# Four sends of the first block moved to ScalarE's queue, and the second clearing of spare rows planned behind the mixing weights

## The chip, the cores and the metric

One core of one Trainium2 chip runs the whole kernel. The metric is the device time of one execution in microseconds (us). Before the change the median of three runs is 1155.92 us (1154.21 to 1157.16).

## The reference

Three layers follow each other: attention in which the heads are mixed before and behind the softmax, then two MLPs. All in float32.

```python
scores = scale * np.matmul(q, k.transpose(0, 1, 3, 2))      # 4 batches, 12 heads, 448 x 448, head size 64
scores = np.einsum('bhij,hg->bgij', scores, w_pre)
scores = scores - np.max(scores, axis=-1, keepdims=True)
attn = np.exp(scores)
attn = attn / (np.sum(attn, axis=-1, keepdims=True) + 1e-09)
attn = np.einsum('bhij,hg->bgij', attn, w_post)
out = np.matmul(attn, v)
...
h = x @ w_in;  x = (h * np.cos(h)) @ w_out                  # 1792 tokens, 768 -> 2048 -> 768
h = max(x @ w1, x @ w2, x @ w3);  x = h @ w_out2            # 768 -> 768 -> 768
```

## The kernel before, in words

The attention is cut into 16 blocks of 100 to 120 queries of one batch (10 to 12 slots of ten queries), four blocks to a batch. Block n goes through these steps, by the names of the program:

- `qk` (L553): for each of six pairs of heads TensorE makes scores for the block's queries in two PSUM tiles. In block 0 the pairs take their tiles from three pools in turn, `ps`, `aps` and `mps`; later all take `ps`, which has two.
- `evac` (L461): ScalarE or VectorE copies each head's scores to SBUF, into one of seven tiles `s`, or in block 0 for odd heads into one of six tiles `e`.
- `send` (L567): a DMA puts one head's scores into the block's grid `t`, so that the heads of one query come to lie on neighbouring partitions. There are two grids, used in turn. Twelve sends fill one. Rows that no send writes must be zero: `fill` (L499) clears them once per grid on GpSimd.
- `mix1` (L576): TensorE mixes the heads with the weight `w`. One visit covers two slots (one slot at the end of a block of 11), so a block has five or six visits, and all blocks 92, numbered 0 to 91. A block's first visit needs all twelve of its sends.
- `rowmax` (L584, VectorE), `soft` (L590, ScalarE's exp with the sum), `guard`, `recip` and `wscale` (L595 to L604, VectorE) make the softmax's parts of a visit; the weight of the second mix, `w2t`, takes the reciprocal in.
- `mix2` (L617): TensorE's second mix of a visit, 64 small matmuls; `keep` (L461) copies the result into a tile `a`.
- `av` (L640): for every one or two blocks, the weighted sums of the values, in three parts; `keepx` and `out` (L655) put them to DRAM.

Before all this `wget` (L507, L509) loads the small weights by GpSimd's queue, and `wmix` (L515 to L522) makes `w` (its step 0) and `w2t` (its step 1) from them on VectorE.

Little of the order is written out by hand. `Plan.add` enters each step with a rank, the engines that may do it with a cost for each (T, A, V, P for TensorE, ScalarE, VectorE and GpSimd; D for SyncE's queue), the steps that it comes after, and the buffers that it takes and frees. `Plan.run` then goes through the steps greedily: of those that by its own clock can start soonest it takes the one of lowest rank, on the engine that would be done first, and writes that instruction into the engine's stream. So a cost or a dependence changed at one place can change the order of everything behind it, and which of two engines makes a copy. The semaphores are set from the data that the instructions share: a dependence that only the plan knows makes no wait in the program. Every engine goes through its stream in order.

The first MLP's matmuls begin among the last visits; the MLPs (L157 to L159) follow.

Of the kernel before, what the change touches and what calls it, by code (L numbers as in the profile page):

```python
# [16 lines left out]
B, H, S, D = 4, 12, 448, 64  # L17
# [30 lines left out]
@with_exitstack  # L48
def talking_heads_mlps(ctx, tc, q, k, v, w_pre, w_post, same_row, w_in, w_out, w1, w2, w3, w_out2, outT):
    nc = tc.nc  # L50
    dram = ctx.enter_context(tc.tile_pool(name="dram", bufs=1, space=bass.MemoryType.DRAM))
    xT = dram.tile([DM, NT], F32, name="xT")

    tp = ctx.enter_context(tc.tile_pool(name="t", bufs=2, side="right", reuse_waits="tile"))
    mlps = Mlps(ctx, tc, xT, tp, w_in, w_out, (w1, w2, w3), w_out2, outT)
    mlps.kept = {(i, f): dram.tile([128, DM], F32, name=f"w{i}_{f}") for i in range(3) for f in range(KC)}
    mlps.kept_out = dram.tile([KC, 128, DM], F32, name="w3")
    mlps.kept.update({(3, f): mlps.kept_out[f] for f in range(KC)})
    with tc.manual_schedule(), ExitStack() as att:
        attention(att, tc, q, k, v, w_pre, w_post, same_row, xT, tp, mlps)  # L60
# [384 lines left out]
def attention(ctx, tc, q, k, v, w_pre, w_post, same_row, xT, tp, mlps):  # L445
# [35 lines left out]
    score, halves = [], []  # L481
# [59 lines left out]
    def score_bank(n, hp):  # L541
        grid = lambda: ps_t.tile([128, JB, H, RI], F32, name="aps").rearrange("p j g i -> p (j g i)")[:, :S]
        return (("ps", lambda: ps_x.tile([128, S], F32, name="ps")), ("ps_t", grid),
                ("ps_m", lambda: ps_m.tile([128, S], F32, name="mps")))[hp % 3 if n == 0 else 0]
# [11 lines left out]
    def copy_place(n, h):  # L556
        return ("e", ep) if n == 0 and h in range(1, 2 * BUFS["e"], 2) else ("s", sp)
# [71 lines left out]
    def pairs(x):  # L629
        return 2 * x, 2 * x + 1  # L630
# [28 lines left out]
    def add(f, a, rank, engines, after=(), turn=False, behind=(), **kw):  # L659

        key = f.__name__, *a
        plan.add(key, rank, partial(f, *a), engines, after, behind=list(before.get(f, ()) if turn else ()) + list(behind), **kw)
        if turn:
            before[f] = [key]
# [9 lines left out]
    for x in range(3):  # L674
        add(wget, (x,), -70.0, {"P": 1.1 + 1.1 * (x == 2)}, lands=3.0)
    for n in range(2):
        add(fill, (n,), -60.0, {"P": 5.0})
    add(wmix, (0,), -39.0, {"V": 0.8}, [("wget", 0), ("wget", 2)])
    add(wmix, (1,), -39.0, {"V": 0.2}, [("wget", 1), ("wget", 2)])
    for n in range(NS):  # L680
        b = score[n][0]
        start, end = score[n - 1][0] != b or not n, n == NS - 1 or score[n + 1][0] != b
        for hp in range(HP):
            r = (first[n - 1] + 0.5 + 0.125 * score[n - 1][3] * hp) if n else -40.0 + hp
            if start:
                early = 8.0 if b else 20.0
                add(qget, (b, hp), r - early, {"D": 0.6}, turn=True, takes=["q"], lands=2.5)
                add(kget, (b, hp), r - early, {"D": 0.6}, turn=True, takes=["k"], lands=2.5)
            ring = score_bank(n, hp)[0]
            add(qk, (n, hp), r, {"T": 0.78}, [("qget", b, hp), ("kget", b, hp)], turn=True, takes=[ring] * 2,  # L690
                frees=[(f, (f + "get", b, hp)) for f in "kq"] if end else [])
            for h in range(2 * hp, 2 * hp + 2):
                add(evac, (n, h), r, {"A": 0.42, "V": 0.53}, [("qk", n, hp)], turn=True, lands=0.16, takes=[place := copy_place(n, h)[0]], frees=[(ring, ("qk", n, hp), h % 2)])
                if h == 0:
                    plan.add(("new_t", n), r, lambda _: None, {}, [("evac", n, 0)], takes=["t"])
                add(send, (n, h), r, {"D": score[n][2] / 125.0}, [("evac", n, h), ("new_t", n)], turn=True, frees=[(place, ("evac", n, h))], lands=3.5)


    for y, (n, t, slots) in enumerate(visits):
# [3 lines left out]
            frees=[("t", ("new_t", n))])  # L703
        for a in range(2):
# [6 lines left out]
            frees=[("e", key("soft", a)) for a in range(2)] + [("w2s", key("wscale"))])  # L711
        for c in slots:
            begin = n == halves[score[n][4]][4][0] and t == c == 0
            add(keep, (y, c), i + 1.5, {"A": 0.45, "V": 0.57}, [key("mix2")], turn=True, lands=0.17, takes=["a2"] * begin,
                frees=[("ps_t", key("mix2"), c)])


    for half, (b, _, _, _, members) in enumerate(halves):
# [5 lines left out]
        for x in range(HP // 2):  # L724
            r = last + 2.5 + 3.0 * x
            for hp in pairs(x) if halves[half][1] == 0 else ():
                add(vget, (b, hp), r - 10.0, {"D": 0.8}, [("send", 0, H - 1)], turn=True, takes=["v"], lands=3.0)
            add(av, (half, x), r, {"T": 0.2 + 0.0139 * halves[half][3]}, [("vget", b, hp) for hp in pairs(x)] + ends, turn=True, takes=["ps_t"],
                frees=[("a2", start)] + [("v", ("vget", b, hp)) for hp in pairs(x) if halves[half][1] + halves[half][2] == S],
# [15 lines left out]
    def put(f, a, rank, engines, after=(), tags=(), late=True, **kw):  # L745

        key = f.__name__, *a
        rings, after, behind = [], list(after), list(kw.pop("behind", ()))
        for tag in tags:
            n, of = PLACES[tag]  # L750
            rings.append((tag, not late or counts[tag] % of < n))
            counts[tag] += 1
            behind += [x for x in taker.get(tag, []) if x != key]
            taker[tag] = [key]
        if not all(early for _, early in rings):
            (behind if tags == ["ps"] else after).append(("open_late",))
        plan.add(key, rank, partial(f, *a), engines, after, takes=rings, behind=behind, **kw)
        return [(key, r) for r in rings]
# [149 lines left out]
    for j in range(2 * FG * NG):  # L908
        fg, i = divmod(j, 2 * FG)
        for x in range(2):  # L910
            if j < FG + 1:
                r = r0 + RANK["fw"] + (2 * j + x) * RANK["fwgap"]
            else:
                r = base(4 * (fg - 1) + i) + 3.0 * x if fg else base(1) - 9.0 + x
# [28 lines left out]
    for n in range(2):  # L943
        r = (r0, N - 1)[n] + RANK[("fx", "x1")[n]]
# [54 lines left out]
    for n in range(2, NB):  # L999
        put(xget, (n,), base(n - 1) - 1.0, {"D": 3.6}, [("hidden", 1, 0, 0)] * (n > 2), tags=["x"], lands=3.0)  # L1000
        for c in range(KC):
            r = base(n) - 3.0 + c * 0.4
# [101 lines left out]
    for u, (l, (j, wi)) in enumerate(units):  # L1104
# [8 lines left out]
        for i, (name, (eng, _, needs)) in enumerate(live["U", u][1].items()):  # L1113
            kind, x = name
            tags = ["wf"] if kind == "get" and x != "S3" else []
            if kind == "high" and parted % 2 == 0:
                tags = ["w"]
            r = urank(u) - 2.0 + i * 0.2 if u else base(last + 2) + 1.0 + i * 0.4
            h = put(unit_weight, (u, name), r, WTIME[eng], [("unit_weight", u, key) for key in needs]
                    + ([("unit_weight", u - 1, ("high", "S4"))] if name == ("high", "11") and u else []),  # L1120
                    tags=tags, lands=3.0 if eng == "D" else 0.0)
# [102 lines left out]
```

## Time and profile before

| | |
|---|---|
| median of three runs | 1155.92 us (1154.21 to 1157.16) |
| the profiled execution, its own time | 1158.33 us |
| its span in the trace | 1156.5 us |
| TensorE busy | 1124.7 us, 97% |
| VectorE busy | 979.4 us, 85% |
| ScalarE busy | 667.0 us, 58% |
| GpSimd busy | 76.0 us, 7% |
| granted TensorE clock over the span | 0.992 |

The profile is of one execution. Its time is 1.83 us more than its span, for what lies around the span. Busy time of TensorE is a sum over matmuls whose ends are modelled, so a full TensorE may still wait inside. PE stands for TensorE, PEld for its weight loads, DVE for VectorE, ACT for ScalarE, POOL for GpSimd, SP for SyncE; a q behind a name means the engine's queue of instructions, where DMAs are issued. The granted clock is the share of TensorE's full 2.4 GHz.

### The profile page before, as it was taken

To read this page: it belongs to the slowest core of one execution; us is meant where nothing else is said; L and a number is where in the kernel's file an instruction comes from. 1 tells how busy PE (TensorE), PEld (TensorE's weight loads), DVE (VectorE), ACT (ScalarE), POOL (GpSimd) and SP (SyncE) were. 2 spreads that over 40 slices of the span, in tenths; PEclk is the share of its full clock that TensorE was granted. 3 is DMA by queue.
4 is the path that set the end of the run, shared out by engine and by line. 5 is a ranking of instruction groups with operands and counts; after the bars stand their busy time and mean duration, and the time that the engine had idled before them with its cause. 6 is when DMAs were issued, how large, how long until landed. Compare 5 with 4: busy or idle time off the path is not lost.

```text
span 1156.5 us, 29873 instructions
## 1 busy us (share of the span) xinstructions
PE 1124.7 (97%) x12028; PEld 944.2 (82%) x12028; DVE 979.4 (85%) x2057; ACT 667.0 (58%) x1497; POOL 76.0 (7%) x66
## 2 busy tenths in 40 slices
PE   7989999899999999999999999999999999999998
PEld 2667666666657899999999999999999999999987
DVE  5777777777878999999999999998887779778994
ACT  3767666566757776555555555655634454445572
POOL 4000000000004200000000000000001021011110
PEclk8999999999998999999999999999999999999999
DMA  7786665645454654344444444431012211222233
GB/s 228 214 220 191 188 199 160 190 146 155 150 165 123 217 153 147 122 124 121 126 130 124 126 127 122 131 109 35 1 35 83 73 50 35 82 62 69 82 119 114
DMA packets 92426, 146.05 MB, mean 126 GB/s; under 512 B 12192, under 2 KB 75264, under 8 KB 92288
## 3 DMA queue, kind: packets, MB, share of 16 engines
q1 hardware_dynamic: 92032, 144.13, 41.2%
q8 instruction: 94, 1.54, 0.6%
q14 instruction: 44, 0.36, 0.1%
q0 software_dynamic: 256, 0.02, 0.0%
HBM read 84.96 MB, written 20.45 MB: 91 GB/s over the span
## 4 chain that ended last, share of the span: by engine, by line
PE 88%; DVE 6%; DMA 3%; issue 2%; ACT 1%; SPq 0%; DVEq 0%; ACTq 0%
PE ps L157 21%; PE ps L159 21%; PE ps L158 21%; PE aps L617 7%; PE mps L576 6%; PE aps L640 6%; PE ps L553 5%; DVE nm L584 1%; DMA k<-in_k_dram 1%; DMA wraw<-in_w_in_dram 1%; DMA t<-s 1%; DVE xs L461 0%; DVE x L148 0%; DVE s L461 0%; DVE x L334 0%
## 5 line engine op out<-in xcount | busy, mean ns | idle before, releaser
L159 PE MATMUL ps<-x,w 128*128 128x448 f32 x816 | 299.8, 367 | 2.4 <-DVE x L148 1.7
L157 PE MATMUL ps<-x,w 128*128 128x448 f32 x816 | 300.5, 368 | 0.9 <-ACT gh L866 0.6
L158 PE MATMUL ps<-x,w 128*128 128x448 f32 x816 | 299.3, 367 | 0.3 <-DVE w L297 0.3
L159 PEld LDWEIGHTS ps<-x,w 128*128 128x128 f32 x816 | 153.4, 188 | 17.5 <-DVE x L148 3.0
L157 PEld LDWEIGHTS ps<-x,w 128*128 128x128 f32 x816 | 153.3, 188 | 16.5 <-ACT gh L866 1.0
L158 PEld LDWEIGHTS ps<-x,w 128*128 128x128 f32 x816 | 153.3, 188 | 13.8 <-DVE w L297 0.7
L617 PEld LDWEIGHTS aps<-w2s,e 60*64 60x64 f32 x5760 | 118.6, 136 | 48.0 <-issue 28.9
L157 PE MATMUL ps<-gh,w 128*128 128x448 f32 x384 | 140.9, 367 | 0.0
L158 PE MATMUL ps<-gh,w 128*128 128x448 f32 x384 | 140.7, 366 | 0.0
L159 PE MATMUL ps<-gl,w 128*128 128x448 f32 x384 | 140.4, 366 | 0.0
L617 PE MATMUL aps<-w2s,e 60*64 60x60 f32 x5760 | 119.9, 221 | 12.3 <-issue 8.0
L590 ACT ACTIVATE e<-mps,nm 128x448 f32<-128x448 f32 (+1 forms) x184 | 116.4, 645 | 14.0 <-DVE nm L584 11.8
L294 ACT CAST w<-wf 128x384 fp32r<-128x384 f32 x168 | 81.1, 514 | 73.7 <-DVE wf L286 55.1
L584 DVE TENSOR_REDUCE nm<-mps 128x1 f32<-128x448 f32 (+1 forms) x184 | 107.5, 616 | 17.1 <-PE mps L576 15.7
L553 PE MATMUL ps<-k,q 64*64 64x448 f32 (+3 forms) x736 | 101.7, 557 | 4.4 <-ACT s L461 2.0
L576 PE MATMUL mps<-t,w 64*64 64x448 f32 (+1 forms) x720 | 96.5, 562 | 4.6 <-DMA k<-in_k_dram 1.7
L823 DVE TENSOR_TENSOR acc<-ps,acc 128x448 f32<-128x448 f32 x168 | 100.3, 615 | 0.6 <-PE ps L159 0.6
L253 ACT ACTIVATE wf<-wraw 128x384 f32<-128x384 f32 x112 | 61.9, 553 | 56.4 <-DMA wraw<-in_w_out_dram 35.5
L297 DVE TENSOR_TENSOR w<-wf,w 128x384 fp32r<-128x384 f32 x132 | 74.6, 585 | 18.7 <-ACT w L294 17.9
L297 POOL TENSOR_TENSOR w<-wf,w 128x384 fp32r<-128x384 f32 x36 | 41.9, 1171 | 681.8 <-DVE wt L257 373.4
L640 PEld LDWEIGHTS aps<-a,v 128*64 128x64 f32 x960 | 58.8, 138 | 30.6 <-ACT a L461 11.5
L461 ACT COPY a<-aps 128x480 f32<-128x480 f32 x104 | 58.1, 574 | 44.0 <-PE aps L617 43.9
(121 smaller groups left out, 1764.3 us busy)
## 6 DMA issues: line engine op xcount, KB each, us to landing
t<-s SPq DMA_DIRECT2D x96, 210.0 KB
wf<-w SPq DMA_DIRECT2D x96, 192.0 KB
wraw<-in_w_out_dram SPq DMA_DIRECT2D x44, 384.0 KB
wraw<-in_w_dram SPq DMA_DIRECT2D x36, 384.0 KB
wraw<-in_w_in_dram SPq DMA_DIRECT2D x32, 384.0 KB
t<-s SPq DMA_DIRECT2D x48, 192.5 KB
w<-wf SPq DMA_DIRECT2D x48, 192.0 KB
t<-s SPq DMA_DIRECT2D x42, 175.0 KB
```

Source lines behind the costliest of these rows:

```text
L157: mm(w[0], x[0], start=first, stop=False)
L158: mm(w[1], x[0], start=False, stop=False)
L159: mm(w[0], x[1], start=False, stop=last)
L294: return nc.scalar.copy(A[x][0], w())
L297: return eng.tensor_sub(A[x][1], w(), f32(A[x][0]))
L553: nc.tensor.matmul(live["s", n, 2 * hp + g][r:end], live["q", b, hp][half, i0 + r:i0 + end], live["k", b, hp][half], start=True, stop=True)
L576: nc.tensor.matmul(live["m", v, a][64 * y:64 * y + 64], w1[k], grids[n % 2][k, t + y, :], start=True, stop=True)
L584: nc.vector.tensor_reduce(nm, of(v, live["m", v, a]), axis=AX.X, op=ALU.max, negate=True)
L590: nc.scalar.activation(of(v, e), of(v, live["m", v, a]), AF.Exp, bias=live["nm", v, a], scale=1.0, accum_out=live["z", v][:, a:a + 1])
L617: nc.tensor.matmul(live["a", v, y][64 * c:64 * c + 64, j, :, a, :], live["e", v, a][k, o:o + 64], live["w2s", v][k, a], start=True, stop=True)
L640: nc.tensor.matmul(ps[64 * g:64 * g + 64, :m], live["v", b, hp][:, j, g, :], a2[:, j, 2 * hp + g, :m], start=j == 0, stop=j == JB - 1)
L823: return nc.vector.tensor_add(acc, po, acc) if fg else nc.scalar.copy(acc, po)
```

## The change

Two lines of the planner's table. The second clearing (n = 1) is entered as coming after `wmix` 1. Of block 0's twelve sends those of heads 1, 4, 7 and 10 get ScalarE as their engine, with a cost of 0.77 in the plan, and so are issued by ScalarE's queue; all others stay on SyncE's.

```diff
     for n in range(2):
-        add(fill, (n,), -60.0, {"P": 5.0})
+        add(fill, (n,), -60.0, {"P": 5.0}, [("wmix", 1)] * n)
     add(wmix, (0,), -39.0, {"V": 0.8}, [("wget", 0), ("wget", 2)])
     add(wmix, (1,), -39.0, {"V": 0.2}, [("wget", 1), ("wget", 2)])
...
-                add(send, (n, h), r, {"D": score[n][2] / 125.0}, [("evac", n, h), ("new_t", n)], turn=True, frees=[(place, ("evac", n, h))], lands=3.5)
+                add(send, (n, h), r, {"A": 0.77} if n == 0 and h % 3 == 1 else {"D": score[n][2] / 125.0}, [("evac", n, h), ("new_t", n)], turn=True, frees=[(place, ("evac", n, h))], lands=3.5)
```

How it moves instructions, at three places. First GpSimd's stream at the start, with the semaphores that each row waits for, as it stands with the change (`t_136` and `t_137` are the two grids):

```order
L509 DMA wraw_121<-in_w_pre_dram 60x12 [waits DVE_49]
L509 DMA wraw_121<-in_w_pre_dram 60x12
L509 DMA wraw_121<-in_w_post_dram 60x12 x2
L507 DMA blk_122<-in_same_row_dram 60x10 [waits DVE_49]
L507 DMA blk_122<-in_same_row_dram 60x10 x3
L499 MEMSET t_136 4x5376
L499 MEMSET t_137 4x5376
```

Before the change these seven rows are the same, waits included.

Second the start of ScalarE and SyncE. ScalarE's stream before, from its third copy on:

```order
L461 COPY s_207<-mps_199 100x448 [waits PE_49]
L461 COPY s_222<-ps_212 100x448 [waits PE_49]
L461 COPY e_232<-ps_213 100x448 [waits PE_49]
L461 COPY s_236<-aps_226 100x448 [waits PE_49]
L461 COPY s_254<-mps_241 100x448 [waits PE_49]
L461 COPY s_259<-ps_248 120x448 [waits PE_49]
L461 COPY s_271<-ps_264 120x448 [waits DMAHW6_49,PE_49,Activation_49]
L461 COPY s_275<-ps_265 120x448 [waits DMAHW0_49,PE_49,Activation_49]
```

and now:

```order
L461 COPY s_207<-mps_199 100x448 [waits PE_49]
L567 DMA t_136<-e_181 10x10x448 [waits DMAHW5_49,DVE_49]
L461 COPY s_223<-ps_212 100x448 [waits PE_49]
L461 COPY e_233<-ps_213 100x448 [waits PE_49]
L567 DMA t_136<-s_207 10x10x448 [waits DMAHW7_49,Activation_49]
L461 COPY e_247<-aps_228 100x448 [waits PE_49]
L567 DMA t_136<-e_233 10x10x448 [waits DMAHW1_49,Activation_49]
L461 COPY e_259<-mps_242 100x448 [waits PE_49]
L461 COPY s_262<-ps_251 120x448 [waits PE_49]
L567 DMA t_136<-s_257 10x10x448 [waits DMAHW3_49,DVE_49]
L461 COPY s_275<-ps_268 120x448 [waits DMAHW6_49,PE_49]
```

SyncE's stream now, the eight sends of block 0 that it keeps and the first of block 1:

```order
L567 DMA t_136<-s_179 10x10x448 [waits DMAHW4_49,Activation_49]
L567 DMA t_136<-s_193 10x10x448 [waits DMAHW6_49,Activation_49]
L567 DMA t_136<-e_195 10x10x448 [waits DMAHW0_49,DVE_49]
L567 DMA t_136<-e_209 10x10x448 [waits DMAHW2_49,DVE_49]
L567 DMA t_136<-s_223 10x10x448 [waits DMAHW4_49,Activation_49]
L567 DMA t_136<-s_238 10x10x448 [waits DMAHW5_49,DVE_49]
L567 DMA t_136<-e_247 10x10x448 [waits DMAHW6_49,Activation_49]
L567 DMA t_136<-e_259 10x10x448 [waits DMAHW7_49,Activation_49]
L567 DMA t_137<-s_262 10x12x448 [waits DMAHW0_49,Activation_49]
```

Four issues stand among ScalarE's copies. Heads 9 and 11 (`e_247`, `e_259`) are now copied by ScalarE, heads 8 and 10 (`s_238`, `s_257`) by VectorE, whose stream has them right behind the five rows of `wmix`, where heads 9 and 11 were; block 1's head 3 went from ScalarE to VectorE as well. Behind the sixth send, which waits for VectorE, SyncE has two more of block 0.

Third TensorE about the first mix of block 9 (visit 51). TensorE's stream is the same up to visit 31's first mix; from there to the attention's end it is another. Before, around the weighted sums from `a_3009`:

```order
L640 MATMUL aps<-a_3009,v_127 64x230 x8
L640 MATMUL aps<-a_3009,v_128 64x230 x8
L576 MATMUL mps<-t,w_124 64x448 x4
L617 MATMUL aps<-w2s,e 64x12x5 x32
L553 MATMUL ps<-k,q 64x448 x2
L553 MATMUL ps<-k,q 56x448 x2
L576 MATMUL mps<-t,w_124 64x448 x4
L617 MATMUL aps<-w2s,e 64x12x5 x32
L553 MATMUL ps<-k,q 64x448 x2
L553 MATMUL ps<-k,q 56x448 x2
L576 MATMUL mps<-t,w_124 64x448 x4
L617 MATMUL aps<-w2s,e 64x12x5 x32
```

and now, from the second mix of visit 49 on:

```order
L617 MATMUL aps<-w2s,e 64x12x5 x32
L553 MATMUL ps<-k,q 64x448 x2
L553 MATMUL ps<-k,q 56x448 x2
L617 MATMUL aps<-w2s,e 64x12x5 x32
L553 MATMUL ps<-k,q 64x448 x2
L553 MATMUL ps<-k,q 56x448 x2
L553 MATMUL ps<-k,q 64x448 x2
L553 MATMUL ps<-k,q 56x448 x2
L576 MATMUL mps<-t,w_124 64x448 x8
L553 MATMUL ps<-k,q 64x448 x2
L553 MATMUL ps<-k,q 56x448 x2
L576 MATMUL mps<-t,w_124 64x448 x8
```

Before, mixes (L576) and second mixes (L617) alternate, and visit 51's mix, the first of those L576 rows, stands while three more visits wait for their second mix. Now no mix stands between the second mixes of visits 48 to 50; the mixes of visits 51 to 54 follow in two groups. The same happens ahead of visits 46, 69 and 81, the first of blocks 8, 12 and 14.

## Rows read from the trace of the kernel before

**Rows 1.** The page, part 1: busy us by engine, share of the span, instructions
```profile
PE 1124.7 (97%) x12028; PEld 944.2 (82%) x12028; DVE 979.4 (85%) x2057; ACT 667.0 (58%) x1497; POOL 76.0 (7%) x66
```
**Rows 2.** Stretches: length, busy of PE, PEld, DVE, ACT, POOL; PEclk, DMA, GB/s
```profile
110.00:345.00 235.00, 224.49 (x5507) 152.69 (x5500) 176.59 (x477) 151.34 (x418) 0.00 (x0) 0.99 0.56 169
...
400.00:1156.00 756.00, 751.92 (x3677) 689.47 (x3675) 672.14 (x1282) 403.64 (x806) 45.82 (x39) 1.00 0.32 96
```
**Rows 3.** Timeline, start, GpSimd and VectorE: start us, us, what, [idle before <-releaser]
```profile
5.54 9.08 POOL L499 MEMSET t<- 4x5376 f32 x2
...
9.51 0.62 DVE L461 COPY e<-mps 100x448 f32<-100x448 f32 x1 [0.65 <-PE mps L553]
10.05 4.60 DVE L515 TENSOR_SCALAR wraw<-wraw 128x12 f32<-128x12 f32 x1
...
15.18 0.62 DVE L461 COPY e<-aps 100x448 f32<-100x448 f32 x1
...
16.24 0.61 DVE L461 COPY s<-ps 120x448 f32<-120x448 f32 x1
```
**Rows 4.** Timeline of SyncE's queue at the start
```profile
14.15 0.76 SPq L567 DMA_DIRECT2D t<-s  x1
15.82 0.76 SPq L567 DMA_DIRECT2D t<-e  x1
...
17.53 0.76 SPq L567 DMA_DIRECT2D t<-e  x1
18.38 3.31 SPq L567 DMA_DIRECT2D t<-s  x4
```
**Rows 5.** Timeline of ScalarE and PE at the start
```profile
9.47 0.53 ACT L461 COPY s<-mps 100x448 f32<-100x448 f32 x1 [0.74 <-PE mps L553]
...
16.91 0.97 PE L553 MATMUL ps<-k,q 64*64 64x448 f32 x6 [0.98 <-DVE s L461]
...
17.98 0.97 ACT L461 COPY s<-ps 120x448 f32<-120x448 f32 x2 [3.06 <-PE ps L553]
...
18.56 2.19 PE L553 MATMUL ps<-k,q 64*64 64x448 f32 x8 [0.68 <-ACT s L461]
...
22.98 3.27 PE L576 MATMUL mps<-t,w 64*64 64x448 f32 x16
```
**Rows 6.** The table by stretch again, 18 to 25 us
```profile
18.00:25.00 7.00, 5.75 (x28) 2.71 (x32) 0.00 (x0) 2.88 (x6) 0.00 (x0) 0.57 0.66 216
```
**Rows 7.** The chain that ended last, where PE's order begins to differ
```profile
127.19 3.28 PE aps L640 x32
```
**Rows 8.** Timeline of PE: last scores and first mix of blocks 2 and 8
```profile
48.63 0.94 PE L553 MATMUL ps<-k,q 64*64 64x448 f32 x8
...
58.28 0.98 PE L576 MATMUL mps<-t,w 64*64 64x448 f32 x8 [1.01 <-DMA t<-s]
...
175.66 0.97 PE L553 MATMUL ps<-k,q 64*64 64x448 f32 x8
...
182.88 0.98 PE L576 MATMUL mps<-t,w 64*64 64x448 f32 x8
```
**Rows 9.** The chain that ended last: a mix, scores, a second mix without waits
```profile
82.79 0.76 PE mps L576 x8
83.55 0.75 PE ps L553 x8
84.31 0.93 PE aps L617 x64
```
**Rows 10.** Timeline of PE: second mix of visit 0, first mixes of visits 5 and 6
```profile
28.89 1.34 PE L617 MATMUL aps<-w2s,e 60*64 60x60 f32 x58
...
40.52 1.74 PE L576 MATMUL mps<-t,w 64*64 64x448 f32 x16
```
**Rows 11.** A pause of PE: a row of its timeline, a row by stretch
```profile
226.66 0.44 PE L617 MATMUL aps<-w2s,e 60*64 60x60 f32 x10 [2.38 <-issue]
...
224.00:231.00 7.00, 4.62 (x106) 3.12 (x101) 3.02 (x8) 2.35 (x8) 0.00 (x0) 0.76 0.79 212
```

## The prediction, made before the run

> **What bounds the kernel now.** I read the page first. TensorE (PE) is busy for 97% of the span [rows 1]. The table by stretch divides that: from 400 us on PE is busy for 751.92 of 756 us, so there an edit is worth what it does to PE's own work, and this edit does nothing to it. In the attention, 110 to 345 us, PE is idle for 10.5 of 235 us [rows 2]. The edit can act there and in the start, which has to be read by itself.
>
> So next the start, by the timeline of each engine. GpSimd clears the two grids back to back, 9.08 us from 5.54 on. VectorE's first step of the mixing weights begins at 10.05 and ends at 14.65, where the second clearing ends; the PSUM copy just ahead of it, beside the first clearing, took its usual 0.62 us [rows 3]. So the weights, and not the copies, are held by GpSimd. Behind them wait three copies of VectorE, the first at 15.18 and the last at 16.24 [rows 3].
>
> SyncE (SP) then: a send costs it 0.76 us, and between the issue at 14.15 and the one at 15.82 it stands still, because that send waits for VectorE's copy [rows 4]. The queue is thus not full when the wait comes: it is VectorE that is late.
>
> Last PE itself: its scores of block 1 wait 0.98 us for VectorE at 16.91, then 0.68 us for ScalarE at 18.56, and its first mix begins at 22.98 right behind scores, with no wait for a send [rows 5]. From 18 to 25 us the granted clock is 0.57, for the most part the lower of its two levels, 1.2 GHz, behind these waits; VectorE does nothing there [rows 6].
>
> **The clearing.** In the plan the second clearing comes after both steps of the weights. In the program GpSimd's rows are what they were: both clearings follow each other and the second waits for no semaphore (the fence on GpSimd above). The two share no data, so none is made. Cost and gain: 0. VectorE's 4.60 us [rows 3] stay.
>
> **The sends.** Four of twelve leave SP, 4 x 0.76 = 3.0 us of issue [rows 4]. But SP is in order, and head 8, which SP sends, is now copied by VectorE behind the weights, ready about 15.8. Behind it three sends of block 0 are left, heads 8, 9 and 11; before there were three too (heads 9, 10 and 11). So the last one is issued at 17.5 as before and block 1's first at 18.38 as before [rows 4]. Gain: 0. What the earlier sends gain is spent waiting.
>
> By the Trainium skill (DMA: Bandwidth & Descriptors, Issuing engines are not separate DMA queues), issuing from several engines saves the issuing sequencer's time alone, since the transfers interleave on the same DMA engines. By that rule the most to be had is the issue time, and the start would be 3.0 us shorter if SP's issue were what it waits for; by the rows it is not, and the sum takes 0.
>
> ScalarE's new work: no send of ScalarE is in the trace. The nearest rows are SP's of the same transfers: 0.76 us one send, or a fourth of 3.31, 0.83 us, with what lies between [rows 4]; the other end is 0, if an issue doesn't hold up ScalarE's own work. I take 0.76. From 10.0 on, the end of its third copy [rows 5], ScalarE then has three issues (2.3 us) and five copies (2.7 us) up to block 1's head 0, done at about 15.0. PE's next use of it is together with VectorE's copy, done at 16.85 [rows 3], so even at 0.83 each it costs 0. The fourth issue waits for VectorE's copy of head 10, about 16.3, and ends at 17.1, ahead of the copy at 17.98, which waits for PE [rows 5]: 0.
>
> One thing improves. ScalarE copied block 1's heads 2 and 3 one behind the other, 0.97 us from 17.98 [rows 5]; now VectorE, idle there [rows 6], copies head 3. PE's second half of the next scores starts at about 18.6 and not 18.95: **-0.35 us**. The bound on this is 0 (if the last send's landing, whose time the rows don't show, then ends the wait) to -0.43.
>
> **The order of the rest.** The plan is a greedy one, and after these edits it puts the attention in another order from 127 us on [rows 7], up to the end of the attention. The MLPs' matmuls stand in the same order. I count PE's stock: mixes already issued whose second mix is still to come. Before, it lies at 3 or more from visit 5 to 89. Now it falls to 2 at visits 44 to 47 and to 1 at visits 50, 68 and 80, always just ahead of a block's first mix, which waits for twelve sends.
>
> Price of such a wait. From the start of a block's last scores to the start of its first mix it took 7.2 us at block 8 (175.66 to 182.88) and 9.65 us at block 2 (48.63 to 58.28) [rows 8]. I take 7.2 for the length of the path copy, send, landing, since the order changes about block 8 and later. PE's work in between, by 0.75 (scores), 0.93 (second mix) and 0.76 (mix; half for a visit of one slot) [rows 9], comes in the new order to 5.4 us at block 8 (scores, half a mix, then three second mixes and two scores), 6.55 at 9 and 6.6 at 12 and 14; in the old order to 6.2 at 8, 12 and 14, and to over 7.2 at 9, where two weighted sums stand between. So the waits become 1.8, 0.65, 0.6 and 0.6 us (3.65) from 1.0, 0, 1.0 and 1.0 (3.0): **+0.65 us**. At 9.65 each they would be 13.4 in place of 3.0: the upper end, +10.4; the lower is 0.
>
> After each wait PE has one visit in stock and must live on scores and weighted sums while the softmax catches up. The only such place in the trace is the start: 28.89 to 40.52 us, 11.63 us, in which PE has five second mixes, five scores and one mix, 9.16 us: 2.47 us lost [rows 10]. That is the upper end for each of three places (7.4); the lower is 0, since weighted sums of 3.3 us [rows 7] fill most of it now, which they did not there. I take 0.45 each, near the low end for that reason: **+1.35 us**.
>
> Sum: -0.35 + 0.65 + 1.35 = +1.65 us. The profiled execution took 1158.33 us (span 1156.5 and 1.83 around it), 2.4 above the median of 1155.92; on the median the forecast is **1157.6 us**, 0.14% up. A change under 0.3% (3.5 us) can't be told from none here, so the forecast counts as the same.
>
> **Rival, slower: the stock-outs cost their full price.** If the softmax does not catch up, each of the three places costs 2.47: 7.4 - 0.35 + 0.65 = +7.7, 1163.6 us. It decides from 1.1 us per place on (3.3 + 0.3 is past 3.5). A pause can also lower the clock: behind 2.38 us without work, to 226.66, the granted clock of 224 to 231 was 0.76 [rows 11], and 0.24 of 7 us, 1.7, is lost again. For it: three places and not one. Against it: the weighted sums next to them. 0.30 with all that ends over 3.5.
>
> **Rival, faster: the new order sheds idle time.** Of 10.5 us idle [rows 2] and the half-speed stretch [rows 11], some is pauses that the profile puts down to no wait of PE's (2.38 us [rows 11]), and a new order may have them where PE waits anyway. Half of 10.5 shed and the sum's first term: -5.6 us, 1150.3. For it: nothing excludes it. Against: the rows name no wait that the new order takes away, and it has lower stocks. 0.15.
>
> **Rival, faster: the clearing does wait.** Then the weights are made at about 10.3, VectorE's three copies come 4.4 us sooner, and SP's last sends and PE's wait of 0.98 with them. At most these 4.4 us of the start go: 1157.6 - 4.4 is 1153.2 us, and by more than 3.5 below the median only if the new order costs less than forecast. Against it: no wait stands in the program. 0.03. The Trainium skill (SBUF — State Buffer, Who interferes with whom) calls the port pair of VectorE and GpSimd an exclusive lock, held for a whole instruction; by that rule only a real wait helps, and the trace agrees (4.60 us, to the clearing's end).
>
> **How the numbers follow.** Forecast 0.52 (all within 3.5 us), slower 0.30, faster 0.15 + 0.03 = 0.18. The range leaves out about a tenth on each side: 1152.0, with a part of the idle time shed (3.9 under the median), to 1163.0, with the three stock-outs nearly in full. The forecast's own range is 1152.4 to 1159.4.
>
> **What would show it.** GpSimd's clearings again back to back and VectorE's weights again over 4 us; four sends on ScalarE of about 0.76 us; SP's eighth send still near 17.5; PE's first mix at about 22.6. In the attention: PE's waits at the first mixes of blocks 8, 9, 12 and 14 longer by 0.65 us in all, the idle time of 110 to 345 us near 12 us. Weights made at 10.3 would prove the clearing moved; a first mix before 21 us would prove that the sends had bounded the start; an attention that ends earlier than before would prove the order's price wrong in sign.

## The result

The changed kernel takes 1167.28 us (median of 4 runs, 1164.0 to 1168.23) beside 1156.54 for the kernel before: a ratio of 1.0099, with a 95% interval of 1.0075 to 1.0123. It is slower by about 11 us (11.4 by the ratio, 10.7 by the two medians); forecast was 1157.6 us, range 1152.0 to 1163.0. The profiled execution took 1164.0 us (span 1162.2), the fastest of the four.

The profile after, the page's busy times and the table by stretch, with the columns of [rows 1, 2]; the third row answers to [rows 6]:

```profile
PE 1127.1 (97%) x12028; PEld 944.1 (81%) x12028; DVE 985.9 (85%) x2060; ACT 664.9 (57%) x1492; POOL 78.5 (7%) x68
```
```profile
110.00:345.00 235.00, 227.28 (x5528) 152.95 (x5518) 179.66 (x478) 150.47 (x412) 0.00 (x0) 1.00 0.56 168
400.00:1156.00 756.00, 752.38 (x3679) 690.98 (x3680) 674.92 (x1285) 406.41 (x813) 48.21 (x41) 1.00 0.32 96
18.00:25.00 7.00, 5.77 (x32) 2.73 (x36) 0.83 (x2) 2.46 (x5) 0.00 (x0) 0.54 0.65 203
392.00:425.00 33.00, 27.93 (x128) 22.97 (x127) 31.45 (x55) 25.07 (x54) 9.17 (x7) 1.00 0.53 161
```

The kernel before in the last of these stretches:

```profile
392.00:425.00 33.00, 31.13 (x147) 27.36 (x148) 31.62 (x57) 26.40 (x58) 6.50 (x5) 1.00 0.48 143
```

The attention looks better fed than before (227.28 of 235 us busy against 224.49 [rows 2]) and the MLPs as full as before. Only a stretch of 33 us in the first MLP shows a loss: 3.2 us of TensorE's work, at a granted clock of 1.00 in both. So much for one pair of executions. To see more, I cut every profiled execution of this study at the same points of TensorE's work, and compared the time from one point to the next. 19 were taken; the new order's and the old order's are kept apart for each stretch, since most experiments below mix the two:

| stretch of TensorE's work | old order, median us (range, executions) | new order | difference |
|---|---|---|---|
| start, to visit 31's first mix | 125.66 (123.49 to 130.65, 9) | 126.46 (125.08 to 128.62, 6) | +0.8 |
| visits 31 to 62 | 117.81 (114.33 to 120.45, 11) | 120.75 (118.86 to 126.26, 8) | +2.9 |
| visits 63 to 86 | 89.16 (88.97 to 89.94, 11) | 90.18 (89.87 to 91.37, 8) | +1.0 |
| hand-over: the last visits, with matmuls of the first MLP among them | 54.52 (53.64 to 54.90, 10) | 54.87 (54.72 to 56.57, 8) | +0.35 |
| start of the first MLP: third and fourth token tile | 31.40 (30.06 to 31.92, 11) | 34.97 (33.34 to 36.53, 5) | +3.6 |
| the rest of the MLPs | 735.4 | 735.4 | 0 |

(A kernel whose own edit changes a stretch is left out of that row. The two profiles shown have 126.22, 120.42, 89.16, 54.57, 30.76 before and 127.53, 119.19, 89.87, 55.25, 34.97 after: 5.7 us, of which the last stretch makes 4.2.) The differences add up to 8.7 us, or 7.9 without the start, and three quarters of the 8.7 lie in visits 31 to 62 and at the start of the first MLP. Only in that last stretch are the two ranges clear of each other; what blurs visits 31 to 62 is shown in the last section.

**The start.** Timeline of the kernel after, 9 to 27 us, in the columns of [rows 3]; it answers to [rows 3 to 5]:

```profile
5.53 9.09 POOL L499 MEMSET t<- 4x5376 f32 x2
10.11 1.47 ACTq L567 DMA_DIRECT2D t<-e  x1
10.63 4.03 DVE L515 TENSOR_SCALAR wraw<-wraw 128x12 f32<-128x12 f32 x1
11.72 0.79 ACTq L567 DMA_DIRECT2D t<-s  x1
12.55 0.53 ACT L461 COPY e<-aps 100x448 f32<-100x448 f32 x1
12.63 0.79 ACTq L567 DMA_DIRECT2D t<-e  x1
16.36 0.79 ACTq L567 DMA_DIRECT2D t<-s  x1
16.68 1.61 SPq L567 DMA_DIRECT2D t<-e  x2
18.39 4.13 SPq L567 DMA_DIRECT2D t<-s  x4
18.59 1.95 PE L553 MATMUL ps<-k,q 64*64 64x448 f32 x8 [0.63 <-ACT s L461]
22.72 2.77 PE L576 MATMUL mps<-t,w 64*64 64x448 f32 x16
```

The clearings are back to back and the weights take 4.03 us beside the second. ScalarE issues four sends, three at 0.79 us and the first at 1.47, and its copy at 12.55 runs beside one of them. SyncE's last two sends of block 0 end at 18.3 and block 1's first is issued at 18.39, against 18.38 [rows 4]. The first mix is 0.26 us earlier than [rows 5].

**The attention.** TensorE at the first mixes of block 9 (visits 51 to 54), kernel after, a row being start, us, what, and in brackets the idle time before it with what ended it; first its matmuls, then its weight loads:

```profile
209.32 1.17 PE L553 MATMUL ps<-k,q 64*64 64x448 f32 x8 [0.64 <-ACT s L461]
210.13 1.87 PE L576 MATMUL mps<-t,w 64*64 64x448 f32 x16
212.73 2.82 PE L576 MATMUL mps<-t,w 64*64 64x448 f32 x16
```
```profile
212.72 0.19 PEld L576 LDWEIGHTS mps<-t,w 64*64 64x64 f32 x2 [0.76 <-ACT e L590]
213.34 0.20 PEld L576 LDWEIGHTS mps<-t,w 60*64 60x64 f32 x6 [0.43 <-ACT e L590]
213.96 0.19 PEld L576 LDWEIGHTS mps<-t,w 64*64 64x64 f32 x2 [0.42 <-ACT e L590]
214.57 0.20 PEld L576 LDWEIGHTS mps<-t,w 60*64 60x64 f32 x6 [0.43 <-ACT e L590]
```

The same visits in the old order (experiment e1, which has it from visit 31 on):

```profile
200.80 0.98 PE L576 MATMUL mps<-t,w 64*64 64x448 f32 x8
203.85 1.02 PE L576 MATMUL mps<-t,w 64*64 64x448 f32 x8
206.29 1.01 PE L576 MATMUL mps<-t,w 64*64 64x448 f32 x8
208.73 1.01 PE L576 MATMUL mps<-t,w 64*64 64x448 f32 x8
```

A single mix takes 1.0 us. In the new order the second group of 16 takes 2.82: it waits inside, each step for ScalarE's exp (L590) to read the PSUM tile that the next matmuls fill. The matmul row counts those waits as busy; only the weight loads show them. So a busy sum need not fall when the work takes longer. That it even rose from 110 to 345 us is chance: from 127 to 240 us the kernel before had 3.6 us more of pauses that are put down to no wait (last section). Ahead of the first group stands a wait of 0.64 us, for ScalarE's copy of scores and not for a send.

Ahead of the first mixes of blocks 8, 12 and 14 stands no such wait for exp. There second mixes (L617) follow each other, and their weight loads wait some 0.6 us each for copies of earlier results (`a`). What these loads waited for from 240 to 340 us (a row: engine, tile and line, what it waited for, us in all, times, longest), in the kernel before and in the kernel after:

```profile
PEld aps L617 <- ACT a L461: 1.6, 3, 0.7
PEld aps L617 <- DVE a L461: 0.9, 2, 0.6
```
```profile
PEld aps L617 <- ACT a L461: 3.9, 7, 0.7
PEld aps L617 <- DVE a L461: 2.1, 5, 0.6
```

Together 2.5 us against 6.0. The old order in e1, e4, e11 and e12 has 2.6 to 4.0, the new one in e2, e3, e10 and e13 5.9 to 6.6. A weight load can wait while matmuls still run, so these sums are no price; how much of the attention's loss comes from them and how much from exp, no run separates.

**The start of the first MLP.** What TensorE waited for between 380 and 425 us (a row: engine, tile and line, what it waited for, us in all, times, longest), in the kernel before and in the kernel after:

```profile
PE ps L159 <- DVE x L148: 1.0, 1, 1.0
PE ps L159 <- POOL x L148: 0.6, 1, 0.6
```
```profile
PE ps L159 <- POOL x L148: 3.0, 4, 1.0
PE ps L157 <- ACT x L144: 1.6, 3, 0.9
PE ps L159 <- DVE x L148: 0.5, 1, 0.5
```

5.1 us against 1.6: 3.5 more, nearly the whole difference of that stretch. `x` here is the input of the MLP, cut for each 128 rows of a token tile into a high part by ScalarE (L144) and a low part by VectorE or GpSimd (L148). ScalarE's timeline at the first and the sixth cut of the third tile, before, and then after, there with the sixth of the fourth tile too:

```profile
388.68 0.57 ACT L144 CAST x<-x 128x448 fp32r<-128x448 f32 x1 [0.21 <-DMA x<-xT]
393.86 0.57 ACT L144 CAST x<-x 128x448 fp32r<-128x448 f32 x1
```
```profile
391.36 0.57 ACT L144 CAST x<-x 128x448 fp32r<-128x448 f32 x1 [0.62 <-DMA x<-xT]
398.74 0.55 ACT L144 CAST x<-x 128x448 fp32r<-128x448 f32 x1
415.31 0.56 ACT L144 CAST x<-x 128x448 fp32r<-128x448 f32 x1
```

The six cuts are spread over 7.4 us in place of 5.2, and the fourth tile's sixth begins 11.6 us behind its fifth. TensorE's matmuls have the order that they had, but what feeds them has not.

### The profile page after: what moved, and what is told of

Same layout as the page of the kernel before. It is cut to its first block, busy times and chain, and to the rows that moved or that the text cites. A ratio compares the mean times of both kernels' runs of the same rounds, so it can differ in the third digit from the quotient of the medians.

```text
span 1162.2 us, 29868 instructions
## 1 busy us (share of the span) xinstructions
PE 1127.1 (97%) x12028; PEld 944.1 (81%) x12028; DVE 985.9 (85%) x2060; ACT 664.9 (57%) x1492; POOL 78.5 (7%) x68
## 3 DMA queue, kind: packets, MB, share of 16 engines
q8 instruction: 94, 1.54, 0.5%
## 4 chain that ended last, share of the span: by engine, by line
PE 86%; DVE 7%; DMA 3%; issue 2%; ACT 2%; SPq 0%; POOL 0%; DVEq 0%; ACTq 0%
PE ps L157 21%; PE ps L158 21%; PE ps L159 21%; PE aps L617 7%; PE mps L576 6%; PE aps L640 5%; PE ps L553 5%; DMA t<-s 1%; DVE nm L584 1%; DMA k<-in_k_dram 1%; DMA wraw<-in_w_in_dram 1%; DVE s L461 1%; DVE a L461 1%; DVE x L148 1%; DVE wt L265 1%
## 5 line engine op out<-in xcount | busy, mean ns | idle before, releaser
L617 PEld LDWEIGHTS aps<-w2s,e 60*64 60x64 f32 x5760 | 116.8, 136 | 54.4 <-issue 25.5
L617 PE MATMUL aps<-w2s,e 60*64 60x60 f32 x5760 | 121.1, 221 | 14.6 <-issue 5.6
L590 ACT ACTIVATE e<-mps,nm 128x448 f32<-128x448 f32 (+1 forms) x184 | 115.8, 638 | 19.7 <-DVE nm L584 15.3
L576 PE MATMUL mps<-t,w 64*64 64x448 f32 (+1 forms) x720 | 96.6, 561 | 4.7 <-DMA t<-s 3.7
L461 ACT COPY a<-aps 128x480 f32<-128x480 f32 x98 | 55.0, 568 | 48.4 <-PE aps L617 47.9
```

Of the source, the lines that this page charges most:

```text
L576: nc.tensor.matmul(live["m", v, a][64 * y:64 * y + 64], w1[k], grids[n % 2][k, t + y, :], start=True, stop=True)
L590: nc.scalar.activation(of(v, e), of(v, live["m", v, a]), AF.Exp, bias=live["nm", v, a], scale=1.0, accum_out=live["z", v][:, a:a + 1])
L617: nc.tensor.matmul(live["a", v, y][64 * c:64 * c + 64, j, :, a, :], live["e", v, a][k, o:o + 64], live["w2s", v][k, a], start=True, stop=True)
```

## Experiments

My theory after the result: the new order behind visit 31 costs the time, not the four issues, nor the clearing. The rivals: the issues hold up ScalarE; or the start is worse; or the loss is a single bad place. Which line makes the order can be read from the instruction streams: the clearing's line alone leaves every engine's stream as it was, the sends' line alone gives exactly the changed kernel's. All comes from the sends' line. All kernels here compute the whole reference. A ratio is to the kernel before on the same chip, with its 95% interval.

Most runs splice the two orders. The planner is first run twice without emitting, and the steps are then emitted from a list (at the places used, both orders have done the same set of steps; e1, e2 and e12 find the first place by the step's name):

```diff
-    plan.run({...})
+    rings = {...}
+    new = {("send", 0, h): {"A": 0.77} for h in range(1, H, 3)}
+    old, new = plan.run(rings, True), plan.run(rings, True, new)
+    for eng, key in new[:617] + old[617:]:
+        plan.last[eng] = plan.ops[key][1](eng) or plan.last.get(eng)
```

Step 617 is visit 31's first mix, 1201 visit 63, 1635 the end of the score tiles, 1927 the third token tile's first matmul.

**e1, the new start alone** (as above), and **e12**, the same with more rounds:

> Start of the changed kernel (four sends by ScalarE, its copies), and from the first mix of visit 31 on the order of the kernel before, on every engine. Theory O (the other order of the steps from 127 us on, with the hand-over to the first MLP, costs the 11 us): 0 to +2 us against the kernel before, about 1157. Theory S (the start costs it: TensorE's pause of 2.69 us at 38.5 us and what follows it): +3 us or more, 1160 or more. Theory A (issues by ScalarE are dear): +5 us or more, and the time between the first and the fourth issue shows it.

> The same kernel as e1 (the start of the changed kernel, the old order from visit 31 on), with more rounds. If its gain of 0.31% was real: ratio 0.995 to 0.999. If the start's gain is the 0.35 us worked out before: 0.999 to 1.001.

e1: 0.9969 (0.9944 to 0.9995). e12: 1.0012 (0.9982 to 1.0042). The gain of e1 did not come back; the start, with its four issues, is worth nothing that can be measured.

**e2, the new order from visit 31 alone** (`old[:617] + new[617:]`):

> The reverse: start of the kernel before (all sends by SyncE), and from the first mix of visit 31 on the order of the changed kernel. Theory O: +8 to +11 us against the kernel before, 1164 to 1168. Theory S: 0 to +2, since the start is the old one. Theory A: 0.

1.0077 (1.0049 to 1.0105): most of the loss, with none of the four issues on ScalarE.

**e3, the new order with SyncE issuing all sends; e4, the old order with ScalarE issuing the four:**

```diff
-        queue_of[eng].dma_start(grids[n % 2]...
+        nc.sync.dma_start(grids[n % 2]...
```
```diff
-        queue_of[eng].dma_start(grids[n % 2]...
+        (nc.scalar if n == 0 and h % 3 == 1 else nc.sync).dma_start(grids[n % 2]...
```

> The whole order of the changed kernel, but SyncE issues the four sends as well, at their places in the order. Theory O: +8 to +11 us, as the changed kernel. Theory A: 0 to +3, since no send is ScalarE's. Theory S: between them, whatever the start then does; a pause of over 2 us near 38.5 us would come with a loss.

> The order of the kernel before on TensorE, VectorE and GpSimd; of block 0's sends ScalarE issues four, heads 1, 4, 7 and 10, and nothing else is moved. Theory O: 0 to +2 us. Theory A: +5 us or more. If the sends by SyncE had bounded the start, first mix before 22 us and -0.5 to -3 us.

e3: 1.0111 (1.0054 to 1.0169). e4: 0.9994 (0.9975 to 1.0013). The loss goes with the order; the issuing engine costs and gains nothing. e4 also shows how little a wait at the start is worth. Timeline of e4, ScalarE and TensorE, where a copy needs one of the seven tiles `s` that a late send still reads:

```profile
23.62 0.97 ACT L461 COPY s<-ps 120x448 f32<-120x448 f32 x2 [4.91 <-DMA t<-s]
24.20 2.18 PE L553 MATMUL ps<-k,q 64*64 64x448 f32 x8 [4.47 <-ACT s L461]
```

By visit 31 the 4.47 us are made up: 126.51 us to there, against 126.22 before.

**e5 to e8, one stretch each in the new order:** visits 31 to 62 (`old[:617] + new[617:1201] + old[1201:]`), 63 to 86 (1201 to 1635), the hand-over (1635 to 1927), and all behind it (from 1927):

> Only the stretch from the first mix of visit 31 to that of visit 63 (about 127 to 250 us) in the order of the changed kernel; all before and behind it in the old order. Theory M (the loss is in the attention's middle, at the places of low stock): +3 us here and +6 in the next, none behind. Theory H (the loss is at the hand-over from the attention to the first MLP, where VectorE, ScalarE and GpSimd have the last softmax and the conversions at once): 0 to +1 here. By the profiled runs so far: +2.6 us (three runs in the new order took 2.6 us longer for these visits than two in the old one).

> Only the stretch from visit 63's first mix to the point where the score tiles are given up (about 250 to 335 us) in the new order. Theory M: +5 to +7 us. Theory H: 0 to +1. By the profiled runs so far, this stretch and the end of the attention together: +3.8.

> Only the hand-over in the new order: from the point where the score tiles are given up to the first matmul of the third token tile's first product (about 335 to 395 us); it gives more steps of cutting x and of the weights to GpSimd. Theory M: 0 to +1 us. Theory H: +4 to +8, with waits of TensorE of 2.5 us near 350 and 1.7 us near 360 us.

> Only what lies behind (from about 395 us on) in the new order, in which TensorE's order is the old one and the other engines' is not. Theory M: 0. Theory H: 0 to +2. By the profiled runs so far, from 395 to 421 us: +3.6, and nothing behind 421 us.

e5 1.0047 (1.002 to 1.0075), e6 1.0044 (1.0018 to 1.007), e7 1.0042 (1.0021 to 1.0063), e8 1.0056 (1.0035 to 1.0078). No single place holds the loss. But together they make 1.9%, twice the whole, so a splice costs something of its own: in e6 two waits of 1.49 and 1.06 us stand at its two seams. The sizes can't be read as shares.

**e13 and e14, two halves** (`old[:617] + new[617:1635] + old[1635:]` and `old[:1635] + new[1635:]`), one seam fewer per stretch:

> The attention's middle (visit 31 to the point where the score tiles are given up) in the new order, start and all behind it in the old one. By TensorE's finished work in the profiled runs so far, the new order takes 3.4 us longer for visits 31 to 62 and 1.3 longer for 63 to 86: +4 to +5 us against the kernel before, if the parts add. If the splices at the seams had cost, as e6's waits of 1.49 and 1.06 us at its seams suggest: less than e5 and e6 together (+10.6), and about +5 all the same.

> The other half: the old order up to the point where the score tiles are given up, the new one behind it. By the profiled runs: +0.3 us in the hand-over and +3.9 in the 35 us behind it, so +3.5 to +5 us against the kernel before, and with e13 the changed kernel's 11. If the hand-over costs 5 by itself (e7's median): +8 to +10, and more than 11 with e13.

e13 1.0054 (1.0025 to 1.0083), e14 1.0047 (1.0019 to 1.0076). Both parts are slower. Together they make 1.01%, the whole's 0.99%: by the ratios some half of the loss lies in the attention and half in the hand-over and the first MLP's start. That split is rough, since each share may lie anywhere from a fifth to four fifths by its interval, and the plain medians of the same runs (1164.97 and 1162.64 us beside 1154.19) would give 0.93% and 0.73%. e14's waits of 380 to 425 us are, to the digit, the three rows of the kernel after.

**e15, e7 once more:**

> The same kernel as e7 (only the hand-over in the new order). Its profile shows 0.3 us lost in its stretch, its median 5. If the trace is right: 0 to +2 us. If the median is: +4 to +6.

1.0031 (1.0008 to 1.0054): again slower, though its trace gives the hand-over at most 2 us (e7 54.91, e15 56.57 us, old 54.52). A pause that looks dear there is not: this row of e7, a wait for ScalarE's copy of weighted sums (`xs`), stands in a hand-over that lost 0.4 us, and the kernel after has the same.

```profile
356.18 1.15 PE L617 MATMUL aps<-w2s,e 60*64 60x60 f32 x60 [2.58 <-ACT xs L461]
```

Where e7 and e15 lose the rest is open.

**e9, four late steps of the new order moved ahead:**

```diff
+    for key, to in ((("convert", ("w", 0, 1), 5), ("keepx", 8, 5)), (("wscale", 91), ("keep", 90, 0)),
+                    (("xhi", 3, 5), ("act", 2, 0, 2)), (("xlo", 3, 5), ("act", 2, 0, 3))):
+        new.insert(spot(to), new.pop(spot(key)))
```

> The changed kernel's order on all engines, with four steps put elsewhere in it: ScalarE's cast of the first weight block's second half behind its two copies of the weighted sums (it waits 3.5 us for VectorE while TensorE waits for the copies, 2.53 us at 355.65); VectorE's scaling of visit 91's weights ahead of its copy of visit 90's result (1.72 us at 365.84); the last cut of the fourth token tile on ScalarE and on GpSimd as early as its neighbours (0.91 and 0.99 us at 415 and 416.6). If these in-order queues are what TensorE waits for, these pauses fall to under 0.5 us each, and the kernel gains 4 to 5 us on the changed one: +5 to +7 against the kernel before. If the pauses come from the engines' load as a whole, they stay or turn up a step later: +9 to +12.

1.0077 (1.0053 to 1.0102): no gain beyond the interval of the change itself. The pause of the hand-over was gone and came back a step later as four of 0.59, 0.61, 0.57 and 1.48 us (56.22 us for the stretch). The two pauses at the fourth tile's sixth cut (0.91 and 0.99 us in the kernel after) were gone, and the MLP's start fell to 32.68.

**e10, the new order with the low parts of the third and fourth tile cut by VectorE** (7 of 12 move from GpSimd):

```diff
+        eng = "V" if key[0] == "xlo" and key[1] > 1 else eng
```

> The changed kernel's order, but VectorE cuts all of x's third and fourth token tiles, where GpSimd had 7 of the 12 steps. If GpSimd's steps (1.1 to 1.6 us each, and a VectorE step beside one takes 1.5 in place of 0.6) make x late, TensorE's pauses from 392 to 401 us, 3.1 us in all, and from 415 to 418, 1.9, become smaller: -2 to -4 us against the changed kernel. If VectorE has no room for them, the pauses grow: +1 to +4.

1.0086 (1.0056 to 1.0116), the stretch 34.45 us: nothing gained that can be measured. TensorE's waits for `x` were 3.5 us, all of them for VectorE now. They moved with the work, and this run can't tell a slow GpSimd from a full VectorE.

**e17, the last cuts of both tiles early, on ScalarE and GpSimd:**

```diff
+    for key, to in ((("xhi", 2, 5), ("hidden", 2, 0, 0)), (("xlo", 2, 5), ("hidden", 2, 0, 2)),
+                    (("xhi", 3, 5), ("act", 2, 0, 2)), (("xlo", 3, 5), ("act", 2, 0, 3))):
+        new.insert(spot(to), new.pop(spot(key)))
```

> The changed kernel's order, with only the last cut of the third and of the fourth token tile, on ScalarE and on GpSimd, put ahead of other work, about where the old order has them. If ScalarE's place for these two casts is what TensorE waits for at the start of the first MLP: the 35 us behind the hand-over (from the third tile's first matmul to the 81st chunk of x, 34.9 us in the new order, 31.1 in the old) fall to 31 to 32.5, TensorE's waits for x there fall from 5.1 to 1 to 2.5 us, and the whole loses 2.5 to 4 us against the changed kernel: +7 to +9 against the kernel before. If the conversions as a whole are too many for the three engines there: 34 to 36 us, and no gain.

1.0082 (1.0052 to 1.0113). TensorE's waits for `x`, 380 to 440 us of e17, and a row by stretch:

```profile
PE ps L159 <- DVE x L148: 1.6, 2, 1.0
PE ps L159 <- POOL x L148: 1.0, 2, 0.5
```
```profile
407.00:410.50 3.50, 3.35 (x9) 3.01 (x10) 3.43 (x8) 3.50 (x9) 1.10 (x1) 0.51 0.09 15
```

The waits are halved, 5.1 to 2.6 us, and those for ScalarE's high parts are gone, so the place of the two moved cuts is the cause of that half; the cause of the other half is open. The time hardly follows: behind waits of 0.53, 0.54 and 1.04 us close to each other the granted clock fell to 0.51, 1.2 GHz, and half of some 3.4 us was lost again (33.48 us for the stretch). The whole kernel's interval takes in that of the change: the price of the late cuts is seen in the trace, and by e8 and e14, but mending two of them did not give it back.

**e11, the clearing really waits** (the kernel before, one element of `own`, which `wmix` reads last, cleared first on GpSimd); **e16, that and the new start:**

```diff
+        nc.gpsimd.memset(own[:1, 0, :1], 0.0) if n else None
         nc.gpsimd.memset(grids[n][:PAD], 0.0)
```

> The kernel before, and the second clearing made to wait for the mixing weights: ahead of it GpSimd clears one element of the tile that VectorE's last step of the weights reads. The rest stands as before. The weights' first step then takes 0.1 to 0.3 us in place of 4.60, and VectorE's copies of heads 9 and 11 come 4 us sooner. If that stall bounds the start: first mix at 19 to 21 us, -2 to -4.4 us. If TensorE's scores and the sends bound it: first mix 0 to 1 us sooner, 0 to -1 us. If the second clearing, now beside the copies, holds these: 0 to +3.

> What the change's words say, without its new order: four sends by ScalarE, the second clearing behind the mixing weights by a wait that is in the program (as in e11), and the old order from visit 31 on. If the start is worth anything to the end: -1 to -4 us against the kernel before. If TensorE makes it up by visit 31, as e11 and e12 say: -1 to +1.

e11 1.0000 (0.9977 to 1.0023), e16 1.0001 (0.9974 to 1.0028). Timeline of e11, GpSimd, VectorE and TensorE:

```profile
11.03 0.16 DVE L515 TENSOR_SCALAR wraw<-wraw 128x12 f32<-128x12 f32 x1
11.57 0.09 POOL L499 MEMSET own<- 1x1 f32 x1 [1.47 <-DVE w L518]
11.61 4.57 POOL L499 MEMSET t<- 4x5376 f32 x1
12.35 0.62 DVE L461 COPY e<-aps 100x448 f32<-100x448 f32 x1 [0.51 <-PE aps L553]
21.19 1.73 PE L576 MATMUL mps<-t,w 64*64 64x448 f32 x16
```

The weights' step falls from 4.60 us to 0.16 and the first mix comes 1.8 us sooner. Visit 31 comes 1.1 us sooner (125.16 us against 126.22), inside the spread, and the end not at all.

In sum: with the old order behind visit 31 (e4, e11, e12, e16) the ratios lie within 0.12% of 1, their intervals within 0.42%; with the new order from there to the end (the change, e2, e3, e9, e10, e17) they are 0.8 to 1.1% up. No version ran faster than the kernel before, but for e1, whose gain e12 did not repeat.

## Why the prediction was wrong, point by point

**The clearing: right.** Cost and gain 0; the weights still take 4.03 us. The rival in which the clearing waits missed its price as well as its condition: e11 makes the wait real, and of the 4.4 us nothing reaches the end. The Trainium skill (SBUF — State Buffer, Who interferes with whom) calls the port pair an exclusive lock, which the first to issue holds for its whole instruction; the 4.03 us beside the clearing and e11's 0.16 us ahead of it agree.

**The sends and ScalarE's issues: right.** 0.79 us for 0.76 (1.47 for the first), SyncE's next block at 18.39 for 18.38, no cost (e4, e12). The rule of the Trainium skill (DMA: Bandwidth & Descriptors, Issuing engines are not separate DMA queues), by which most was to be had if issue had been the bound, would have given 3.0 us; e4 shows 0.

**-0.35 us at the start: right in place, worth nothing.** Scores at 18.59 (18.6 forecast), first mix at 22.72 (22.6). I carried it through to the end. No run shows that it gets there: e4 loses 4.47 us and e11 wins 1.8 at the same place, and neither shows behind visit 31.

**The order in the attention: right in sign, too small.** Forecast +0.65 and +1.35 us, 2.0 together; the stretches of visits 31 to 86 show +3.9, and e13 +0.54%, some 6 us (2.9 to 9.6). Both terms had the wrong wait. TensorE is not idle for a send at the first mixes of blocks 8, 9, 12 and 14 in either order (a weight load of block 9 waits 0.22 us for one); the row of block 8 in [rows 8], for which I had put 1.0 us, shows no wait either. What the traces show at the places of low stock is not idle time but waits of the weight loads: at block 9 mixes in groups, slowed by the exp that frees their PSUM (2.82 us a group of 16 against 2 x 1.0) and 0.64 us for ScalarE, at the other three second mixes behind copies. That these make up the whole of the attention's loss is argued. My check on it, idle time near 12 us, was the wrong instrument: idle time fell to 7.7 us, as the waits lie inside busy rows and as pauses were missing by chance.

**The step that failed: the sum stopped at the attention's end.** I wrote that from 400 us on "an edit is worth what it does to PE's own work, and this edit does nothing to it", and of the MLPs only that their "matmuls stand in the same order". They do. But the greedy plan moved ScalarE's, VectorE's and GpSimd's steps there too, and at the third and fourth token tile TensorE now waits 3.5 us more for cuts of `x` (+3.6 us by stretches; e8 +0.56%, e14 +0.47%). 751.92 of 756 us busy said how full the stretch was, not how far ahead its feeders were; after the change it is 752.38. With the attention at its measured +3.9 us and nothing behind it, the sum would have come to some 1159.5 us (1155.92 - 0.35 + 3.9), within the range.

**The rivals.** "Stock-outs at full price", 1163.6 us at 0.30, was nearest, right in sign, but by a place that is only half of the story. The faster rival had a true half: pauses put down to no wait do differ (below), but, as far as the traces tell, by the execution and not by the order.

**Open.** Of 11.4 us the stretches locate 7.9 behind the start, and some 9 if visits 31 to 62 are compared at like pauses (next section). The start's 0.8 does not show at the end (e12). Single executions in one and the same order differ by 6 to 7 us in a stretch (114.33 to 120.45, 123.49 to 130.65), and the profiled one of the change was its fastest run; the remaining 2 to 3 us are not located.

## What to carry to other kernels

In a greedily planned kernel, compare the streams of the feeding engines to the end of the program, not only the bounding engine's: the same matmuls in the same order can be starved. Read waits of a pipelined engine from its weight loads too, since its busy time counts them as work. A saving or a loss at the start, with slack of microseconds behind it, is worth nothing until it is seen at a later common point.

## What the runs showed of the hardware

**TensorE pauses, it seems, for its own instructions.** In visits 31 to 62 the waits that the profile puts down to "issue" go with most of the spread between executions of one order. A pause of the kernel after, and the page's row on a queue of the kind "instruction" (packets, MB, share):

```profile
41.19 0.38 PE L617 MATMUL aps<-w2s,e 60*64 60x60 f32 x10 [2.69 <-issue]
```
```profile
q8 instruction: 94, 1.54, 0.5%
```

94 packets make 1.54 MB, 16 KB each; TensorE has 24,056 records, so if they are its own, that makes 64 bytes an instruction and 256 to a packet, an estimate. In the 19 profiled executions there are 117 such pauses. They come back at the same places of TensorE's stream, most of these about a packet's number of instructions apart or a multiple of it, and in 111 of them work resumes 1.2 to 1.8 us behind the end of a packet: in the kernel after the packet runs from 38.37 to 39.60 and work resumes at 41.19; in the kernel before ([rows 11]) the packet ends at 225.11 and work resumes at 226.66. That a late packet is the cause is argued from this; no run tried it. Their size differs from execution to execution. TensorE's waits of 127 to 240 us, before and after:

```profile
PE aps L617 <- issue: 4.3, 2, 2.4
```
```profile
PE aps L617 <- issue: 0.7, 2, 0.4
```

So the very stretch in which the new order is dearer by 2.9 us in the median looks 1.2 us cheaper in the two profiles shown, 119.19 against 120.42. One profile on each side is no measure of a change of 1%. Executions with under 0.8 us of such pauses in visits 31 to 62 took 114.34 to 115.26 us there in the old order (e1, e7, e11) and 118.86 to 119.19 in the new (e5, e13, the change): some 4 us apart and no overlap. At the start the pauses do not carry the spread: e15 took 125.66 us with 3.8 us of them, e7 130.65 with 2.2. In e17 two such pauses, of 2.11 and 2.45 us, each left a granted clock of 0.76 over 7 us, as [rows 11] does:

```profile
145.00:152.00 7.00, 4.89 (x134) 3.51 (x129) 3.67 (x10) 3.41 (x10) 0.00 (x0) 0.76 0.71 188
240.00:247.00 7.00, 4.55 (x88) 2.53 (x82) 3.74 (x12) 3.21 (x9) 0.00 (x0) 0.76 0.36 103
```

**GpSimd's clearing does not hold all of VectorE's work.** Beside it in e11 a PSUM copy keeps its 0.62 us, while the weights' first step (L515) takes 4.03 to 4.60 beside it and 0.16 without. The Trainium skill (SBUF — State Buffer, Who interferes with whom) limits the lock to work that needs the shared port pair; the 0.62 agrees, and which form needs it is shown here for these two alone.
